# One decode step of cached attention and a gated MLP on one core: loops that stay rolled, an output projection in four column groups, and a first pass that does nothing

## The chip, the cores and the metric

The kernel runs on one core of a Trainium2 chip. The metric is device microseconds of one execution. The kernel before took 1302.17 us (median of three runs, 1301.73 to 1303.38). The profiled execution is a further one, and its own time stands beside its span below.

## The reference

Two sequences (B = 2) decode one token each. All numbers are float32.

```
h  = x + attention(layernorm(x)) @ wo        x: 2 x 448, 16 heads of 256
     q = layernorm(x) @ wq                   wq: 448 x 4096
     p = softmax(q . k_cache / 16)           k_cache, v_cache: 2 x 16 x 8192 x 256
     o = p @ v_cache                         wo: 4096 x 448
h2 = h + ((n @ w_gate) * (n @ w_up)) @ w_down    n = layernorm(h), F = 1792
```

The two caches are 537 MB of the 561 MB that have to be read, each byte once.

## The kernel before, in words

There are 32 turns, one for each pair of head and sequence. A turn's keys (8 MB) and values (8 MB) come by two DMAs that SyncE (SP) issues on one queue; 128 partitions hold 64 positions each. VectorE (DVE) multiplies keys by the query, which TensorE and ScalarE (ACT) have spread over the partitions, and sums each position (L334, L337), first 16 positions and then 48. TensorE (PE) transposes the maxima (L422), spreads the top (L426), adds up the exponentials (L431), spreads the query of a later turn (L270) and multiplies values by weights: 32 matmuls of 512 columns (`mix`, L413) whose outputs stand at partitions 0, 32, 64 and 96 in turn, which here are called four column groups. L438 turns the result into columns, and ACT writes it, scaled, into `oT`.

K is double buffered and V single. SP's order is fixed: the keys of turn i+1 go out when the maxima of turn i-1 are done (`m_in`), the values of turn i when the matmuls of turn i-1 are done (event "M"). On PE turns 0 to 30 are a hardware loop (`T.loop`); DVE, ACT and SP are written out turn by turn, and PE's 32nd turn and all that comes behind it are written out too.

The end is a chain. `project_out` multiplies `oT` of heads 0 to 14 by `wo` in two column halves (L493), part of it before and part behind the last turn's softmax. When the last values are in, head 15 follows: `o_sb` (L560), L438, `oT` (L563), eight matmuls into `h_ps` (L589), the mean, the centred residual `xr` (L630), the gate projection (L668, needs `wg`), the up projection in two halves (L668, `wu_a` and `wu_b`), their product (L717), transposes (L720, L727) and the down projection into `y_ps`, 14 chunks of four matmuls of 112 columns (L738), behind the four pieces of `wd`. Then a copy (L747) and the output DMA. The residual reaches `y_ps` by L523 and, for head 15, by L697.

Of the kernel before, what the change touches and what calls it, by code (L numbers as in the profile page):

```python
# [3 lines left out]
F32 = mybir.dt.float32  # L4
# [6 lines left out]
P = 128  # L11
HALF = 64
DC = 4
YN, YW = 4, D // 4
HW = D // 2
# [6 lines left out]
LASTV = 48  # L22
# [5 lines left out]
WIDE = [[min(n, (k + 1) * FH) - k * FH for n in FG] for k in range(2)]  # L28
PACKED = [3 * sum(n) + n[0] + n[2] for n in WIDE]
FF = [(n, g) for n in range(4) for g in range(4) if n < FG[g] // P]  # L30
DOWN = (5, 5, 3, 1)
# [8 lines left out]
class Line:  # L40


    def __init__(self, nc, engine, name):
        self.e = engine
        self.sem = nc.alloc_semaphore(name=name)
        self.n = 0
        self.seen = {}

    def wait(self, *tokens):
        for sem, n in tokens:  # L50
            if self.seen.get(sem.num, 0) < n:
                self.e.wait_ge(sem, n)
                self.seen[sem.num] = n

    def did(self, ins):
        ins.then_inc(self.sem, 1)
        self.n += 1
        return self.sem, self.n


class Tensor:


    def __init__(self, nc):
        self.e = nc.tensor
        self.sem = nc.alloc_semaphore(name="pe")
        self.n = 0
        self.parts = [(None, [])]

    def loop(self, *turns):  # L70

        self.parts.append((turns or None, []))

    def do(self, make, *waits, inc=False):
        self.parts[-1][1].append((make, waits, inc))
        if inc:
            self.n += 1
            return self.sem, self.n

    def emit(self):  # L80
        for turns, ops in self.parts:
            if turns:
                with self.e.Fori(*turns) as turn:
                    self.emit_part(ops, turn)
            else:
                self.emit_part(ops, None)

    def emit_part(self, ops, turn):
        seen = {}
        for make, waits, inc in ops:  # L90
            for w in waits:
                sem, n = w[:2]
                if len(w) == 3:
                    self.e.wait_ge(sem, turn * w[2] + n)
                elif seen.get(sem.num, 0) < n:
                    self.e.wait_ge(sem, n)
                    seen[sem.num] = n
            ins = make() if turn is None else make(turn)
            if inc:
                ins.then_inc(self.sem, 1)  # L100


def decode_block(nc, x, k_cache, v_cache, wq, wo, wg, wu, wd, out):
# [6 lines left out]
    bank = [nc.alloc_psum_tensor(f"bank{i}", [P, 512], F32)[:] for i in range(8)]  # L110
    first_sem = nc.alloc_semaphore(name="dve_first")
    V = Line(nc, nc.vector, "dve")
    A = Line(nc, nc.scalar, "act")
    A_q = Line(nc, nc.scalar, "act_q")
    G = Line(nc, nc.gpsimd, "pool")
    S = Line(nc, nc.sync, "sp")
    T = Tensor(nc)

# [11 lines left out]

    room = {"at": 2 * NF * D}

    def late(*shape):

        n = 1
        for k in shape[1:]:
            n *= k
        at = room["at"]
        room["at"] += -(-n // 8) * 8
        assert room["at"] <= NJ * DH  # L140
        got = k_flat[1][: shape[0], at : at + n]
# [15 lines left out]
    xr = sb("xr", P, DC + 1, B, 16)  # L157
    xz = sb("xz", P, DC + 1, B)
    sel = sb("sel", P, 2)
    rep = sb("rep", P, 2, B, REP)  # L160
    q_sb = sb("q_all", B, H * DH)

    s_x, s_wq, s_k0 = landing("x"), landing("wq"), landing("k0")
    s_k = [landing("k_even"), landing("k_odd")]
    s_v, s_v2 = landing("v"), landing("v_last")
    s_wo = [landing("wo_a"), landing("wo_b")]
    s_wg, s_wu = landing("wg"), [landing("wu_a"), landing("wu_b")]
    s_wd = [landing(f"wd{i}") for i in range(len(DOWN))]
    s_out = landing("out")

    def keys_of(cache, i, lo, hi):
        h, b = divmod(i, B)
        return cache[b, h].rearrange("(p j) d -> p j d", p=P)[:, lo:hi, :]

    x_in = load(A, x_sb, x.rearrange("b s d -> (b s) d"), s_x)
    wq_t = v_flat[:, : 3 * H * DH + H * DH // 2]
    wq_in = load(S, wq_t, wq, s_wq)
    k0_in = load(S, k_sb[0][:, :HC], keys_of(k_cache, 0, 0, HC), s_k0)  # L180
    k_in = {0: load(S, k_sb[0][:, HC:], keys_of(k_cache, 0, HC, NJ), s_k[0])}
    k_in[1] = load(S, k_sb[1], keys_of(k_cache, 1, 0, NJ), s_k[1])

    zero = G.did(nc.gpsimd.memset(ident, 0.0))
    G.wait(zero)
    ident_in = G.did(
        nc.gpsimd.affine_select(
            out=ident, in_=ident, compare_op=ALU.not_equal, fill=1.0, base=0,
            pattern=[[-1, P]], channel_multiplier=1,
        )  # L190
    )
    G.did(nc.gpsimd.memset(xz, 0.0))
    zeros_in = G.did(nc.gpsimd.memset(xr[:, DC - 1 :], 0.0))
# [12 lines left out]
    V.wait(t)
    xc_sb = sb("xc", B, DC * P)
    t = V.did(nc.vector.tensor_scalar(xc_sb[:, :D], x_sb, xmean, None, op0=ALU.add))
    V.wait(t)
    xc_in = V.did(nc.vector.tensor_copy(xc_sb[:, D:], xc_sb[:, D - HALF : D]))  # L210
    xq = o_sb[:B, :D]
    t = V.did(nc.vector.tensor_mul(xq, xc_sb[:, :D], xc_sb[:, :D]))
    V.wait(t)
    xvar = sb("xvar", B, 1)
    var_in = V.did(nc.vector.tensor_reduce(xvar, xq, axis=AX.X, op=ALU.add))

    std = sb("std", B, 1)
    A.wait(var_in)
    std_in = A.did(nc.scalar.activation(std, xvar, AF.Sqrt, bias=eps_t, scale=1.0 / D))
    rstd = sb("rstd", B, 1)  # L220
    V.wait(std_in)
    rstd_in = V.did(nc.vector.reciprocal(rstd, std))
    A.wait(rstd_in)
    A.did(nc.scalar.activation(std, std, AF.Exp, scale=0.0))

    xT_ps = bank[3][:, : DC * B].rearrange("p (c b) -> p c b", b=B)
    for c in range(DC):
        xT_in = T.do(
            lambda c=c: nc.tensor.transpose(
                xT_ps[:, c, :], xc_sb[:, c * P : (c + 1) * P], ident[:B, :B]  # L230
            ),
            ident_in, xc_in, inc=c == DC - 1,
        )
    V.wait(xT_in, zeros_in)
    for rows, c, to in LAYOUT:
        xz_in = V.did(nc.vector.tensor_copy(xz[rows, to], xT_ps[rows, c]))

    V.wait(ident_in)
    V.did(
        nc.vector.tensor_reduce(  # L240
            sel, ident.rearrange("p (g r) -> p r g", r=32)[:, :2, :], axis=AX.X, op=ALU.add
        )
    )
    V.did(
        nc.vector.tensor_copy(
            rep,
            ident.rearrange("p (k b) -> p k b", k=2)[:, :, :B, None].to_broadcast([P, 2, B, REP]),
        )
    )
    for ps in (o_ps, h_ps, bank[4][:, :HW]):  # L250
        set_in = V.did(nc.vector.memset(ps, 0.0))

    q_sel = sb("q_sel", B, DH)
    qb = [sb(f"qb{i}", P, DH) for i in range(2)]
    qb_ps = bank[1][:, :DH]
    q_ps = [bank[7][:B, :], bank[4][:B, :]]
    qsel_in, qb_in, Q_in = {}, {}, {}

    def select(i):
        h, b = divmod(i % NQ, B)  # L260
        if i > 0:
            A.wait(Q_in[i - 1])
        qsel_in[i] = A_q.did(
            nc.scalar.activation(  # L264
                q_sel, q_sb[:, h * DH : (h + 1) * DH], AF.Copy, scale=ident[:B, b : b + 1]
            )
        )

    def spread_query(*_):
        return nc.tensor.matmul(qb_ps, ones[:B, :], q_sel, start=True, stop=True)  # L270

    def take_query(i):
        A.wait(Q_in[i])
        qb_in[i] = A_q.did(nc.scalar.activation(qb[i % 2], qb_ps, AF.Copy))  # L274

    q_in = {}
    for g in range(NG):
        for c in range(DC):
            xs = c if c < DC - 1 else c + g // (NG // 2)
            at = c * H * DH + (g * QG if c < DC - 1 else g % (NG // 2) * QG)  # L280
            done = T.do(
                lambda g=g, c=c, xs=xs, at=at: nc.tensor.matmul(  # L282
# [11 lines left out]
        if g == 0:  # L294
            A.wait(q_in[0])
            select(0)
        if g == 1:
            Q_in[0] = T.do(spread_query, qsel_in[0], set_in, inc=True)
# [519 lines left out]
```

## Time and profile before

| | |
|---|---|
| median of three runs | 1302.17 us |
| profiled execution | 1301.42 us, span 1300.1 us |
| busy: DVE, PE, ACT | 1131.2, 470.6, 81.5 us |
| 16 DMA engines, mean busy share | 99.7% on the data queue |
| PE's granted clock, mean | 0.64 |

The profile's chain of waits gives 74% of the span to DMA and 25% to PE, nearly all of the latter `mix`. A timeline row has start and length in us, engine, line, operation, tiles, shapes and count; a float32 matmul is two records. In brackets stands how long the engine had been idle, and what ended that.

### The profile page before, as it was taken

The page shows a single profiled execution, that of the slowest core. Times are in us where ns is not written, and L with a number is a line of the kernel's source. Part 1 is how long each engine was busy: PE and PEld are TensorE (multiplying, and loading weights), DVE is VectorE, ACT ScalarE, POOL GpSimd, SP SyncE. Part 2 cuts the span into 40 slices and gives each one's busy share as a digit, 9 for nine tenths or more (in the row PEclk, how much of TensorE's full clock was granted, in tenths as well). Part 3 has the DMA queues.
Part 4 walks back from the last instruction along what each step waited for, and adds up shares of the span by engine and source line. Part 5 has one row for each costly group of instructions (what it writes and reads, how often), then busy time and mean ns, then how long its engine had stood idle before and what let it go on. Part 6 is the DMA issues. An engine that isn't in the chain of part 4 may idle for free.

```text
span 1300.1 us, 6914 instructions
## 1 busy us (share of the span) xinstructions
PE 470.6 (36%) x2992; PEld 155.1 (12%) x2992; DVE 1131.2 (87%) x266; ACT 81.5 (6%) x239; POOL 0.8 (0%) x8
## 2 busy tenths in 40 slices
PE   3643224333323433322333322333321333432387
PEld 0111011101001101101101101101100110110123
DVE  1999998889888889888889988888988888988861
ACT  1100000000000000000000000000000000000000
POOL 0000000000000000000000000000000000000000
PEclk9866566666556666556666656666656666655689
DMA  9999999999999999999999999999999999999998
GB/s 411 427 450 421 450 421 444 426 436 436 421 450 421 448 423 448 423 446 425 442 427 427 444 421 450 422 446 425 446 423 446 425 440 429 427 444 423 446 421 367
DMA packets 10973, 561.31 MB, mean 432 GB/s; under 512 B 1234, under 2 KB 1364, under 8 KB 1492
## 3 DMA queue, kind: packets, MB, share of 16 engines
q1 hardware_dynamic: 10960, 561.19, 99.7%
q8 instruction: 5, 0.08, 0.0%
q14 instruction: 4, 0.03, 0.0%
q10 hardware_dynamic: 4, 0.00, 0.0%
HBM read 561.19 MB, written 0.00 MB: 432 GB/s over the span
## 4 chain that ended last, share of the span: by engine, by line
DMA 74%; PE 25%; issue 0%; ACT 0%; SPq 0%; DVE 0%
DMA v<-in_A_v_cache_dram 71%; PE bank L413 22%; PE bank L282 2%; DMA v<-in_wd_dram 2%; DMA v<-in_wq_dram 1%; PE bank L270 0%; SPq L123 0%; PE bank L738 0%; ACT q_all L290 0%; ACT q_sel L264 0%; DVE k L747 0%; ACT qb L274 0%
## 5 line engine op out<-in xcount | busy, mean ns | idle before, releaser
L334 DVE TENSOR_TENSOR k<-k,qb 128x4096 f32<-128x4096 f32 x64 | 555.3, 8676 | 124.2 <-DMA k<-in_A_k_cache_dram 95.9
L337 DVE TENSOR_REDUCE s<-k 128x16 f32<-128x4096 f32 x64 | 555.2, 8675 | 1.1
L413 PE MATMUL bank<-v,p 128*2 128x512 f32 x2048 | 291.4, 733 | 342.9 <-DMA v<-in_A_v_cache_dram 342.9
L413 PEld LDWEIGHTS bank<-v,p 128*2 128x2 f32 x2048 | 53.6, 96 | 573.4 <-DMA v<-in_A_v_cache_dram 365.9
L426 PE MATMUL bank<-nm,row 1*128 1x1 f32 x64 | 18.4, 354 | 227.6 <-DVE nm L343 227.6
L422 PE MATMUL bank<-ident,m 128*1 128x128 f32 x32 | 11.8, 368 | 184.4 <-DVE m L381 184.4
L363 ACT ACTIVATE o_sb<-bank 128x512 f32<-128x512 f32 x31 | 18.5, 597 | 604.0 <-PE bank L413 604.0
L426 PEld LDWEIGHTS bank<-nm,row 1*128 1x128 f32 x64 | 15.6, 302 | 236.9 <-DVE nm L343 236.9
L438 PE MATMUL bank<-sel,o_sb 128*128 128x1 f32 x256 | 33.7, 253 | 23.3 <-ACT o_sb L363 22.5
L270 PE MATMUL bank<-q_sel,ones 2*128 2x256 f32 x66 | 39.0, 691 | 1.4 <-ACT q_sel L264 1.4
L438 PEld LDWEIGHTS bank<-sel,o_sb 128*128 128x128 f32 x256 | 31.0, 191 | 53.1 <-ACT o_sb L363 51.5
L282 PE MATMUL bank<-v,xz 128*2 128x512 f32 x64 | 30.7, 639 | 16.0 <-DMA v<-in_wq_dram 16.0
L352 ACT ACTIVATE nb<-bank 128x1 f32<-128x1 f32 x32 | 5.5, 171 | 441.5 <-PE bank L426 441.5
L431 PE MATMUL bank<-lsum,ones 128*128 128x1 f32 x64 | 18.5, 359 | 23.5 <-ACT p L355 23.5
L422 PEld LDWEIGHTS bank<-ident,m 128*1 128x1 f32 x32 | 2.5, 79 | 188.2 <-DVE m L381 187.8
L431 PEld LDWEIGHTS bank<-lsum,ones 128*128 128x128 f32 x64 | 15.8, 306 | 26.2 <-ACT p L355 26.2
L270 PEld LDWEIGHTS bank<-q_sel,ones 2*128 2x128 f32 x66 | 15.9, 297 | 3.7 <-ACT q_sel L264 2.4
L264 ACT ACTIVATE q_sel<-q_all,ident 2x256 f32<-2x256 f32 x33 | 16.2, 492 | 0.0
L274 ACT ACTIVATE qb<-bank 128x256 f32<-128x256 f32 x32 | 12.2, 382 | 54.5 <-PE bank L270 54.5
L493 PE MATMUL bank<-k,oT 128*2 128x224 f32 x120 | 13.4, 387 | 0.0
L343 DVE TENSOR_REDUCE nm<-bank 1x1 f32<-1x128 f32 x32 | 8.7, 272 | 4.4 <-PE bank L422 4.4
L597 DVE TENSOR_REDUCE k<-bank 128x1 f32<-128x128 f32 x1 | 0.3, 292 | 13.1 <-PE bank L589 13.1
(81 smaller groups left out, 97.3 us busy)
## 6 DMA issues: line engine op xcount, KB each, us to landing
v<-in_wq_dram SPq DMA_DIRECT2D x1, 7168.0 KB, 19.5
k<-in_wo_dram SPq DMA_DIRECT2D x2, 3584.0 KB, 35.3
k<-in_A_k_cache_dram SPq DMA_DIRECT2D x1, 6144.0 KB, 38.0
v<-in_A_v_cache_dram SPq DMA_DIRECT2D x1, 6144.0 KB, 21.6
k<-in_wg_dram SPq DMA_DIRECT2D x1, 3136.0 KB, 28.0
v<-in_wd_dram SPq DMA_DIRECT2D x2, 1120.0 KB, 18.0
k<-in_A_k_cache_dram SPq DMA_DIRECT2D x1, 2048.0 KB, 23.9
v<-in_A_v_cache_dram SPq DMA_DIRECT2D x1, 2048.0 KB, 26.1
```

The source lines that it names most:

```text
L264: nc.scalar.activation(q_sel, q_sb[:, h * DH : (h + 1) * DH], AF.Copy, scale=ident[:B, b : b + 1])
L270: return nc.tensor.matmul(qb_ps, ones[:B, :], q_sel, start=True, stop=True)
L282: lambda g=g, c=c, xs=xs, at=at: nc.tensor.matmul(q_ps[g % 2], xz[:, xs, :], wq_t[:, at : at + QG], start=(c == 0), stop=(c == DC - 1),),
L334: t = V.did(nc.vector.tensor_mul(kt, kt, q[:, None, :].to_broadcast([P, hi - lo, DH])))
L337: V.did(nc.vector.tensor_reduce(s_t[i % 2][:, lo:hi], kt, axis=AX.X, op=ALU.add)),
L363: osb_in[i] = A.did(nc.scalar.activation(o_sb, o_ps, AF.Copy))
L413: lambda *_, t=t, g=g: nc.tensor.matmul(o_ps[g : g + 2, :], p_t[:, 2 * t : 2 * t + 2], v_sb[:, 2 * t : 2 * t + 2, :], start=(t < 4), stop= ...
L422: return T.do(lambda *_: nc.tensor.transpose(mT_ps, m_t, ident), m, inc=True)
L426: lambda *_: nc.tensor.matmul(nb_ps, row, nm, start=True, stop=True), nm_done, inc=True
L431: lambda *_: nc.tensor.matmul(l_ps, ones, lsum, start=True, stop=True), p_done, inc=True
L438: lambda *_, c=c, k=k: nc.tensor.matmul(oT_ps[:, c : c + 1], o_sb[:, (2 * k + c) * P : (2 * k + c + 1) * P], sel[:, k : k + 1], start=(k = ...
L493: lambda h=h, c=c, k=k: nc.tensor.matmul(acc_ps[HALF * k : HALF * k + B, :], oT[:, h, c, :], wo_c[:, h, c, k * HW : (k + 1) * HW], start=F ...
```

## The change

1. An `Engine` class replaces `Line` and `Tensor`: work is listed with the names it waits for, and loops are emitted rolled. DVE: 15 passes of two turns; ACT: 16 passes of two; PE: 32 turns, with the work of the last turn behind branches inside the loop (`only`); the query projection: 4 passes of two groups.
2. PE, DVE and ACT each put their program into a loop of two passes, of which the first branches over everything (`early`, with a branch hint at the back edge). On PE that loop ends behind the gate projection, on the other two at the program's end.
3. Output projection: `acc_ps` is 448 wide, head h goes to column group h % 4. `wo` is one DMA, not two. Head 15 goes into the same bank; ACT copies the sum out with a running total, and four matmuls with `sel` add the groups while they transpose. The separate `h_ps` path, L523 and L697 are gone.
4. The up projection is whole, its two halves of product, transpose and copy follow it. `wu` is cut by rows and not by columns.
5. Down projection: the first ten chunks are 448 wide in column groups (`part_ps`); DVE adds them to the residual (`both`), and four matmuls with `rep` bring that into `y_ps` between chunk 11 and chunk 12. `wd` comes in five pieces and not four, and waits for the whole of the last `mix` and not for its first three quarters.

```diff
+    def emit(self, known):
+        seen = {}
+        if self.split:
+            with self.nc.Fori(0, 2, 1, engines=[self.e.engine], hint_back_edge=True) as go:
+                with self.e.If(go > 0):
+                    self.emit_ops(self.items[: self.split], known, seen)
+        self.emit_ops(self.items[self.split :], known, seen)
...
-DOWN = (5, 5, 3, 1)
+DOWN = (5, 5, 2, 1, 1)
+NPART, OPEN_AFTER = 10, 11
...
+    scores(0)
+    V.roll(1, NQ - 1, 2, lambda i: (scores(i), scores(i + 1)))
+    scores(NQ - 1)
...
+    A.roll(0, H, 1, act_turn)
...
+    def project_out(heads, *waits, done=None):
+        for c in range(2):
+            for h in heads:
+                g = 32 * (h % 4)
+                T.do(
+                    lambda h=h, c=c, g=g: nc.tensor.matmul(
+                        acc_ps[g : g + B, :], oT[:, h, c, :], wo_c[:, h, c, :],
+                        start=(h < 3 and c == 0), stop=(h >= H - 4 and c == 1),
...
+            project_out(range(0, 4), "wo", ("oT", H - 1))
...
+    project_out([H - 1], ("oT", NQ - 1), done="acc")
+    A.do(
+        lambda: nc.scalar.activation(sums[:, :D], acc_ps, AF.Copy, accum_out=total),
...
+                xc_ps[:, c, :], sums[:, c * P : (c + 1) * P], sel, start=(c == 0), stop=False
...
+    project(g_ps, wg_t, lambda c: "wg", "g", "g_blank", variance)
+    T.early()
...
+    project(u_ps, wu_t, lambda c: ("wu", c // 2), "u", "u_blank")
...
+                part_ps[32 * (k % 4) : 32 * (k % 4) + B, :],
+                hmT[:, j, 32 * g : 32 * (g + 1) : REP], wd_t[:, k, :],
...
+        lambda: nc.vector.tensor_tensor(both, part_ps, sums[:, :D], op=ALU.add),
```

PE between the 31st turn's end and the last `mix`, before: the projection of heads 0 to 7 (L493) waits for the first half of `wo`.

```order
L438 MATMUL bank<-sel,o_sb 128x1 [waits act] x4
L83 REGISTER_ALU
L83 COMPARE_AND_BRANCH
L482 MATMUL bank<-x,ident 2x224 x2
L493 MATMUL bank<-k,oT 2x224 [waits act,wo_a]
```

The same place now, inside the loop (L121 is the branch, L528 the projection, L557 the transposed maxima).

```order
L121 COMPARE_AND_BRANCH
L540 MATMUL bank<-x,ident 2x448
L528 MATMUL bank<-k,oT 2x448 [waits act0,wo]
L528 MATMUL bank<-k,oT 2x448 x15
L121 UNCONDITIONAL_BRANCH
L140 ISA
L557 MATMUL bank<-ident,m 1x128 [waits dve0]
```

The projection has half as many matmuls, twice as wide, and waits for all of `wo`; the last turn's softmax (from L557) still stands behind it.

PE behind the last `mix`, before: L438 to the first matmul of the gate projection.

```order
L438 MATMUL bank<-sel,o_sb 128x1 [waits act]
L438 MATMUL bank<-sel,o_sb 128x1 x3
L589 MATMUL bank<-k,oT 2x128 [waits act]
L589 MATMUL bank<-k,oT 2x128 x7
L613 MATMUL bank<-k,ones 128x8 [waits dve]
L620 MATMUL bank<-ident,k 128x8 [waits act]
L668 MATMUL bank<-k,xr 32x512 [waits dve,wg]
```

The same place now: L581 is the old L438, L528 head 15, L605 the sum over column groups, L615 the mean, L662 the gate projection.

```order
L581 MATMUL bank<-sel,o_sb 128x1 [waits act0]
L581 MATMUL bank<-sel,o_sb 128x1 x3
L106 REGISTER_ALU
L106 COMPARE_AND_BRANCH
L528 MATMUL bank<-k,oT 2x448 [waits act0]
L528 MATMUL bank<-k,oT 2x448
L605 MATMUL bank<-sel,k 128x2 [waits act0]
L605 MATMUL bank<-sel,k 128x2 x2
L605 MATMUL bank<-sel,k 128x2 [waits dve0]
L615 MATMUL bank<-k,ones 128x8 [waits dve0]
L662 MATMUL bank<-k,xr 32x512 [waits dve0,wg]
```

Eight narrow matmuls in four column groups became two wide ones in one group, and the two small ones behind them became five.

## Rows read from the trace of the kernel before

**Rows 1.** The page: data queue, packets, MB, share of 16 engines.
```profile
q1 hardware_dynamic: 10960, 561.19, 99.7%
```
**Rows 2.** Waits, 100 to 1200 us: total us, times, longest us.
```profile
PE bank L413 <- DMA v<-in_A_v_cache_dram: 316.3, 28, 12.0
DVE k L334 <- DMA k<-in_A_k_cache_dram: 92.3, 27, 3.9
```
**Rows 3.** DMA issues, whole span: count, median us from issue to landing.
```profile
k<-in_A_k_cache_dram SPq DMA_DIRECT2D x31, 42.1
v<-in_A_v_cache_dram SPq DMA_DIRECT2D x31, 29.5
```
**Rows 4.** Timeline of the head: `wq` is in, and the first values go out.
```profile
20.32 9.78 PE L282 MATMUL bank<-v,xz 128*2 128x512 f32 x16 [16.02 <-DMA v<-in_wq_dram]
53.66 0.33 SPq L123 DMA_DIRECT2D v<-in_A_v_cache_dram  x1
```
**Rows 5.** DMA queues, 100 to 1200 us: the only packets of code.
```profile
q14 instruction: 4, 0.03, 0.0%
```
**Rows 6.** DMA queues, 1240 to 1301 us: packets of code on PE's queue.
```profile
q8 instruction: 4, 0.07, 0.4%
```
**Rows 7.** Timeline of the end, from the last but one `mix`.
```profile
1238.73 9.86 PE L413 MATMUL bank<-v,p 128*2 128x512 f32 x64 [11.63 <-DMA v<-in_A_v_cache_dram]
...
1250.78 7.91 PE L493 MATMUL bank<-k,oT 128*2 128x224 f32 x64
...
1260.67 5.46 PE L493 MATMUL bank<-k,oT 128*2 128x224 f32 x56
...
1270.35 7.05 PE L413 MATMUL bank<-v,p 128*2 128x512 f32 x64 [3.11 <-DMA v<-in_A_v_cache_dram]
...
1277.46 0.60 ACT L560 ACTIVATE o_sb<-bank 128x512 f32<-128x512 f32 x1 [17.15 <-PE bank L413]
...
1279.20 0.26 ACT L563 ACTIVATE oT<-bank,rl 128x2 f32<-128x2 f32 x1 [1.14 <-PE bank L438]
...
1279.52 0.62 PE L589 MATMUL bank<-k,oT 128*2 128x128 f32 x16 [0.35 <-ACT oT L563]
...
1280.75 0.39 PE L613 MATMUL bank<-k,ones 128*128 128x8 f32 x2 [0.61 <-DVE k L604]
...
1281.40 0.57 DVE L630 COPY xr<-bank 128x96 f32<-128x96 f32 x3 [0.60 <-PE bank L620]
...
1282.58 0.20 PEld L668 LDWEIGHTS bank<-k,xr 128*32 128x32 f32 x8 [1.31 <-DMA k<-in_wg_dram]
1282.59 3.29 PE L668 MATMUL bank<-k,xr 128*32 128x512 f32 x16 [1.22 <-DVE k L643]
...
1286.12 1.91 PE L668 MATMUL bank<-k,xr 128*32 128x512 f32 x16
...
1291.37 1.06 PE L668 MATMUL bank<-k,xr 128*32 128x256 f32 x16
...
1292.51 0.42 DVE L717 TENSOR_TENSOR k<-bank,k 128x256 f32<-128x256 f32 x1 [0.61 <-PE bank L668]
1292.99 0.44 PE L720 MATMUL bank<-ident,k 128*128 128x128 f32 x2 [0.56 <-DVE k L717]
...
1296.95 0.97 PE L738 MATMUL bank<-v,k 128*32 128x112 f32 x32 [0.46 <-DMA v<-in_wd_dram]
1298.00 0.28 DVE L747 COPY k<-bank 128x112 f32<-128x112 f32 x1 [4.11 <-PE bank L738]
```
**Rows 8.** Windows of the end: busy us of each engine, PE's granted clock, DMA share, GB/s.
```profile
1270.00:1272.00 2.00, 1.65 (x16) 0.42 (x20) 0.00 (x0) 0.00 (x0) 0.00 (x0) 1.00 1.01 434
1282.00:1284.00 2.00, 1.41 (x10) 0.69 (x14) 0.88 (x5) 0.00 (x0) 0.00 (x0) 0.50 1.04 444
...
1295.00:1296.00 1.00, 0.67 (x28) 0.68 (x32) 0.00 (x0) 0.00 (x0) 0.00 (x0) 1.00 0.69 274
1296.00:1297.00 1.00, 0.54 (x26) 0.30 (x19) 0.00 (x0) 0.00 (x0) 0.00 (x0) 1.00 0.29 113
```

More of the change, by code (lines that the diff above doesn't have):

```diff
@@ L37 @@
 )
[L40 to L84, printed above, removed]
-            else:
[L86 to L100, printed above, removed]
@@ L168, in decode_block @@
[L168 to L181, printed above, removed]
@@ L223, in decode_block @@
[L223 to L236, printed above, removed]
@@ new lines, in decode_block @@
+    G.do(lambda: nc.gpsimd.memset(xz, 0.0))
+    G.do(lambda: nc.gpsimd.memset(xr[:, DC - 1 :], 0.0), done="blanks")
+    for t, value in ((eps_t, EPS), (ones, 1.0), (avg, 1.0 / D), (row, DH**-0.5)):
+        V.do(lambda t=t, value=value: nc.vector.memset(t, value))
+    V.do(
+        lambda: nc.vector.tensor_reduce(xsum, x_sb, axis=AX.X, op=ALU.add), "x", done="xsum"
+    )
+    V.do(
+        lambda: nc.vector.tensor_scalar(xmean, xsum, -1.0 / D, None, op0=ALU.mult),
+        "xsum", done="xmean",
+    )
@@ new lines, in decode_block, with spread_query @@
+    V.do(
+        lambda: nc.vector.tensor_reduce(
+            sel, ident.rearrange("p (g r) -> p r g", r=32)[:, :2, :], axis=AX.X, op=ALU.add
+        ),
+        "ident", done="sel",
+    )
+    V.do(
+        lambda: nc.vector.tensor_copy(rep, sel[:, :, None].to_broadcast([P, B, REP])), "sel"
+    )
+    zeroed = (o_ps, part_ps, acc_ps)
+    for ps in zeroed:
+        V.do(lambda ps=ps: nc.vector.memset(ps, 0.0), done="set" if ps is acc_ps else None)
+    GH = NG // 2
+    def spread_query(i, name="Q"):
+        T.do(
+            lambda *_: nc.tensor.matmul(qb_ps, ones[:B, :], q_sel, start=True, stop=True),
+            ("qsel", i), done=(name, i),
+        )
@@ new lines, in project_groups @@
+    def project_groups(t):
+        for k in range(2):
+            for c in range(DC):
+                xs, base = (c, c * H * DH + k * GH * QG) if c < DC - 1 else (c + k, c * H * DH)
+                T.do(
+                    lambda turn, k=k, c=c, xs=xs, base=base: nc.tensor.matmul(
+                        q_ps[k], xz[:, xs, :], wq_t[:, bass.ds(turn * QG + base, QG)],
+                        start=(c == 0), stop=(c == DC - 1),
+                    ),
+                    *([("q", 2 * (t - 1) + k)] if c == 0 else []),
+                    done=("qp", 2 * t + k) if c == DC - 1 else None,
+                )
+        T.only(t == 0, spread_query, 0, "Q0")
@@ L402, in every, with collect @@
-    def every(tokens):
-        sem, n = tokens[0]
-        by = tokens[1][1] - n
-        assert all(tokens[i] == (sem, n + by * i) for i in range(TURNS)), tokens
-        return sem, n, by
-    def mix(lo, hi, landed):
+            ),
+            ("nb", i), done=("p", i),
+        )
+    def collect(i, turn_of):
+        b = i % B
+        A.do(lambda *_: nc.scalar.activation(o_sb, o_ps, AF.Copy), ("M", i), done=("osb", i))
+        A.do(
+            lambda turn: nc.scalar.activation(
+                oT[:, bass.ds(turn_of(turn), 1), :, b], oT_ps[:, None, :], AF.Copy, scale=rl
+            ),
+            ("O", i), ("rl", i), done=("oT", i),
+        )
@@ L410, in mix, with act_turn @@
+    def act_turn(h):
+        for b in range(B):
+            i = h * B + b
+            exponentials(i)
+            take_query(i + 2)
+            select(i + 3, lambda turn, b=b: (turn + (b + 3) // B) & (H - 1))
+            collect(i, lambda turn: turn)
+    A.roll(0, H, 1, act_turn)
+    def mix(i, lo, hi, *waits, done=None):
         for t in range(lo // 2, hi // 2):
             g = 32 * (t % 4)
-            done = T.do(
+            T.do(
                 lambda *_, t=t, g=g: nc.tensor.matmul(
@@ new lines, in heads_out, with hold, tensor_turn @@
+    def heads_out(k):
+        if k == 0:
+            T.do(
+                lambda: nc.tensor.matmul(
+                    acc_ps[3 * 32 : 3 * 32 + B, :], ident[:B, :B], x_sb, start=True, stop=False
+                )
+            )
+            project_out(range(0, 4), "wo", ("oT", H - 1))
+            project_out(range(4, 8))
+        else:
+            project_out(range(8, 12), ("oT", NQ - 3))
+            project_out(range(12, H - 1))
+    def hold(*waits):
+        T.do(None, *waits)
+    def tensor_turn(i):
+        last = i == NQ - 1
+        T.only(last, heads_out, 0)
+        T.do(
+            lambda *_: nc.tensor.transpose(mT_ps, m_t, ident), ("m", i), done=("T", i)
+        )
+        T.do(
+            lambda *_: nc.tensor.matmul(nb_ps, row, nm, start=True, stop=True),
+            ("nm", i), done=("N", i),
+        )
+        T.do(
+            lambda *_: nc.tensor.matmul(l_ps, ones, lsum, start=True, stop=True),
+            ("p", i), done=("L", i),
+        )
+        spread_query(i + 2)
+        T.only(last, heads_out, 1)
+        at = 0
+        for k, n in enumerate(LAST):
+            if k > 0:
+                T.only(last, hold, ("v_last", k))
+            mix(
+                i, at, at + n, *([("v", i)] if k == 0 else []),
+                done=("M", i) if k == len(LAST) - 1 else None,
+            )
+            at += n
@@ L545, in decode_block @@
-    last["M"] = mix(LASTV, NJ, v2_in)
-    S.wait(mixed_a)
-    wd_t = v_flat[:, : NF * D].rearrange("p (n d) -> p n d", d=D)
-    wd_in, at = {}, 0
-    for k, cnt in enumerate(DOWN):
-        got = load(
-            S, wd_t[:, at : at + cnt, :].rearrange("p n d -> p (n d)"),
-            wd[:, at * D : (at + cnt) * D], s_wd[k],
-        )
-        for j in range(at, at + cnt):
-            wd_in[j] = got
-        at += cnt
-    A.wait(last["M"])
-    osb_in[n] = A.did(nc.scalar.activation(o_sb, o_ps, AF.Copy))
@@ L627, in decode_block @@
+            "sums", *(["sums_d"] if c == DC - 1 else []),
+        )
+    V.do(
+        lambda: nc.vector.tensor_mul(mean, share, total[:, None, :].to_broadcast([P, DC, B])),
+        "sums", "share", done="mean",
+    )
+    T.do(
+        lambda: nc.tensor.matmul(xc_ps, ones, mean, start=False, stop=True), "mean", done="xc_h"
+    )
     for rows, c, to in LAYOUT:
         k = rows.stop - rows.start
-        xr_in = V.did(
-            nc.vector.tensor_copy(
+        V.do(
+            lambda rows=rows, c=c, to=to, k=k: nc.vector.tensor_copy(
@@ new lines, in decode_block @@
+    down_of = [k for k, n in enumerate(DOWN) for _ in range(n)]
+    for k, (j, g) in enumerate(FF[:NPART]):
+        T.do(
+            lambda k=k, j=j, g=g: nc.tensor.matmul(
+                part_ps[32 * (k % 4) : 32 * (k % 4) + B, :],
+                hmT[:, j, 32 * g : 32 * (g + 1) : REP], wd_t[:, k, :],
+                start=(k < 4), stop=(k >= NPART - 4),
+            ),
+            ("hmT_in", j // 2), ("wd", down_of[k]), done="part" if k == NPART - 1 else None,
+        )
+    both = late(P, D)
@@ L722, in product, with open_sum @@
+    V.do(
+        lambda: nc.vector.tensor_tensor(both, part_ps, sums[:, :D], op=ALU.add),
+        "part", "sums", done="both",
+    )
+    def open_sum():
+        for q in range(DC):
+            T.do(
+                lambda q=q: nc.tensor.matmul(
+                    y_ps[32 * q : 32 * q + 32, :], rep.rearrange("p b r -> p (b r)"),
+                    both[:, q * W : (q + 1) * W], start=False, stop=False,
                 ),
-                t, inc=j == 1,
+                "both",
             )
-        V.wait(flipped)
@@ new lines, in decode_block @@
+        if k == OPEN_AFTER:
+            open_sum()
+    y = late(P, W)
+    V.do(lambda: nc.vector.tensor_copy(y, y_ps), "y", done="y_in")
+    s_out = landing("out")
+    load(S, out, y[::REP, :], s_out, "out", "y_in")
+    S.do(lambda: nc.sync.sem_clear(range(first_sem.num, s_out.num)))
+    S.do(lambda: nc.sync.sem_clear(s_out), "out")
+    engines = (S, A, G, V, T)
+    for e in engines:
+        e.count(known)
+    known["all_q"] = known["qp", NG - 1]
+    A.early()
+    V.early()
+    for e in (S, G, T, A, V):
+        e.emit(known)
```

828 lines of the change are left out of this document (371 added, 457 removed).

## The prediction

> **What bounds the kernel now.** I read the DMA part of the page first, because the chain of waits is three quarters DMA. The data queue kept the 16 engines busy for 99.7% of the span [rows 1], and 561.19 MB in 1300.1 us are 0.432 MB a us. Next come the waits of the steady part: per turn PE waits 11.3 us for values (316.3 / 28) and DVE 3.4 us for keys (92.3 / 27) [rows 2]. Then the issues, which say whether the queue ever runs dry: 8.39 MB need 19.4 us, yet values land 29.5 us after their issue and keys 42.1 us after theirs [rows 3]. So a value DMA stands 10 us, a key DMA 23 us behind other data, and the stream doesn't notice an engine that is later by less. In such a kernel a change can act in three places only: before the stream starts, on the stream's own length, and behind its last byte. The end is read from the timeline [rows 7] and from the windows [rows 8].
>
> **Steady turns.** Rolled loops add register instructions for waits and a branch per pass. No row prices them. Their cover is DVE's 3.4 us a turn, 6.8 us a pass of two turns, and PE's 11.3 us; ACT is busy 81.5 us in all. A row bounds them from above in kind: PE ran 31 passes of such a loop, and its only long waits in it are for data [rows 2]. Lower end 0, upper end (refetched code) is a rival below; I take 0, nearest to PE's loop. Writing out fewer turns removes nothing that anyone waited for either.
>
> **Head.** The empty passes, the new order on DVE and the register addresses of the query projection all lie before or in a stretch with cover: PE stands idle 16.0 us until `wq` lands at 20.32 [rows 4]. Behind it the price of lateness is the first values' issue at 53.66: 7.34 + 16.78 MB are ahead of it, which at 0.432 MB a us plus about 2 us of start end near 58, so some 4 us are free, less the lead that a transfer needs. The 32 matmuls stay the same; one of the two query spreads goes behind them. I take 0; an empty pass would have to cost over 16 us, or the loop over 3 us, to show.
>
> **Stream.** Bytes are the same. `wo` in one piece saves one DMA, the fifth piece of `wd` adds one: nothing. `wd` now waits for all of the last `mix`, some 2 us later; 6.4 MB of `wg` and `wu` are ahead of it, 14.8 us, so its place in the queue is free. One thing can change. In the last 61 us PE's queue brought four packets of code that took 0.4% of 16 engines, so 3.9 us or 1.0 us of one engine each [rows 6]; an engine that carries one is late with its own data for good. And the engines do end raggedly: shares of 0.69 and 0.29 in the last two us [rows 8]. If the empty pass loads the tail's code early, up to (1 - 0.69) + (1 - 0.29) = 1.0 us can come back. If early packets only move the lateness, 0. I take 0 and keep -1.0 as a bound, because the early packets fall on the same engines' first data.
>
> **Behind the last turn's keys.** The projection of heads 0 to 7 started at 1250.78, on the first half of `wo` [rows 7]. It now waits for the whole. `wo` is complete when the last values' first part starts: 6.29 MB take 14.6 us and were used at 1270.35, so 1255.7. Its 16 matmuls of 448 columns run in four column groups, as `mix` does: 7.05 us for 32 of 512 is 0.22 each, 0.19 for 448 columns, 3.1 us; at the low clock at most double, 6.2. The softmax behind it keeps the 2.0 us between the two L493 rows, the extra query spread costs up to 1.2, and 14 more matmuls 2.7 to 5.3. PE is ready between 1264.2 and 1270.4; the values were used at 1270.35. Hidden, though its upper end just touches.
>
> **From the last values to the gate projection.** This is the path. `o_sb` to `oT` keeps its instructions (+0.1 for a register address). Head 15: eight matmuls in four groups took 0.62; now two of 448 columns stand in one group, one behind the other, so 4 x 0.19 = 0.75 each, 1.5 us at the full clock and 3.0 at the low one: +0.9 to +2.4. The copy of the sum is 448 columns and a running total where before a total and a 128-column copy ran in a row: `o_sb`, 512 columns, takes 0.60, so 0.6 to 0.8 against 0.6: 0 to +0.2. Four matmuls with `sel` are what L438 is (1.14 us that `oT` waited), then one of 0.39, against the old stretch from 1280.75 to 1281.40: +0.6 to +0.9. The three copies to `xr` stay. Sum: +1.6 to +3.6, likeliest +1.9, so `xr` is ready at 1281.97 + 1.9 = 1283.9. Before, the gate projection started at 1282.59, held by `wg`. It is late by 1.3 us, bounds 1.0 and 3.0.
>
> **From there to the end.** The gate projection took 5.4 us, from 1282.59 to 1288.03, at 0.50 in its first half [rows 7, 8]. Now to 1289.3. L697's eight matmuls on PE are gone, and the up projection is 16 matmuls at about 0.22, 3.5 us: 1292.8, against 1292.43 before (1291.37 + 1.06). `wu`'s second half was needed near 1290 before and is no later. Then both products (0.42 each), transposes (0.44) and copies (0.42): the first copy is done 1.5 us after the up projection, the second 2.0. Ten chunks at 0.19 take 1.9 us from 1294.3 to 1296.3; DVE adds 448 columns, 0.42 x 448 / 256 = 0.7, to 1297.0; the four `rep` matmuls and the last eight cost 0.5 to 0.7: 1297.7. Before, PE ended at 1297.92, after a wait of 0.46 for `wd` [rows 7]. So compute arrives when the data does: the last chunk can't start before its piece lands near 1297.3, and the end stays at 1297.9, -0.5 to +2.0. The final copy (0.28) and the output DMA stay.
>
> The sum is 0: the profiled execution would again take 1301.4, of which 1300.1 are span. It lay 0.75 below the median of the runs, and that spread (1301.73 to 1303.38) is as large as my terms; I put the forecast on the median, 1302.2.
>
> **Rivals.** *The clock falls before the last `mix` (slower).* PE had paused 3.1 us and still had 1.00 when the values came [rows 7, 8]. In the new order PE's work behind the softmax may end near 1267 or earlier, with no L523 work behind it, so the pause may be longer. A steady `mix`, which begins at the low clock after 11.6 us of pause, took 9.86 against 7.05 [rows 7]: +2.8. No wait is left in the chain to absorb it, except the 0.2 us above, and head 15 at the low clock adds up to 1.5. Price +1.8 to +4, centre +2.4: 1304.6. It decides from a pause at which the granted clock has gone to 0.50. For it: after the quiet stretch ahead of 1282 the clock did fall. Against it: the pause may be no longer, and a slower last `mix` is possible before as well, so part of it is in the old median. Chance 0.22.
>
> *The engines' ragged end is evened out.* -1.0 at the last landing, if compute is also early enough (full clock in the gate projection saves 3.29 - 1.91 = 1.4). 1301.2. Chance 0.17.
>
> *Loops fetch their code again.* If every back edge did, 16 on ACT, 15 on DVE and 31 on PE bring 62 packets of 1.0 us on 16 engines: 3.9 us on the stream, 1306.1, and more where a stall exceeds 6.8 us a pass on DVE. Against it: while PE's loop turned 28 times, between 100 and 1200 us, its queue brought no packet at all [rows 5]. [...] This trace doesn't show it for PE, and none shows a loop on ACT or DVE. It decides if a loop doesn't stay loaded. Chance 0.04.
>
> *Faster by more than the ragged end holds.* I see no mechanism; 0.02 for one that I have missed.
>
> **How the numbers follow.** The forecast, no change within a microsecond, has 0.55. Taking 0.2% (2.6 us) as what a measurement of this kernel can tell from none: the slow clock passes it in about a third of its cases, 0.08; with refetching 0.04 slower has 0.12. Faster has 0.03, same 0.85. The range, from 1300.8 (ragged end) to 1304.9 (slow clock, most of it), leaves out about 0.15. The likeliest case's own range is 1301.2 to 1303.2.
>
> **What would show it.** Right: the data queue near 99.7%, `mix` still waiting about 11 us for values, no code packets in the steady part; `xr` near 1284, so that `wg` no longer ends PE's wait there; the last down matmuls on `wd` or within a microsecond of it. Wrong: a DVE wait for something other than keys, a share of the data queue under 99%, a last PE matmul that ends behind 1299 with its clock at 0.50 in the last `mix`, or an end before 1296.5.

## The result

The changed kernel took 1303.59 us (median of 22 runs, 1301.72 to 1307.58), the kernel before beside it 1301.76 (22 runs, 1301.35 to 1303.38). The ratio is 1.0015, 95% interval 1.0008 to 1.0021: slower by 0.15%, inside the 0.2% that the prediction took as no change, but clear of noise. The spread tells more than the median. Nine of the 22 executions lie between 1301.7 and 1302.3, where most of the kernel before lie (18 of 22 are under 1302.4); six between 1303.0 and 1304.6; seven between 1306.1 and 1307.6. The profiled execution is one of the last: 1306.09 us, span 1304.8.

First the rows that answer to [rows 1, 2] and the wait that [rows 4] showed: data queue and q8 (page; read as PE's code queue, as four of its five packets in the kernel before came behind 1240 [rows 6], where PE leaves its loop near 1250), the only row of the DMA queues from 100 to 1200 us, waits from 100 to 1200 us, and the start.

```profile
q1 hardware_dynamic: 10960, 561.19, 99.4%
q8 instruction: 2, 0.03, 0.0%
```
```profile
q1 hardware_dynamic: 8193, 477.17, 100.1%
```
```profile
PE bank L515 <- DMA v<-in_A_v_cache_dram: 318.8, 28, 11.6
...
DVE k L426 <- DMA k<-in_A_k_cache_dram: 95.1, 27, 3.8
```
```profile
2.22 0.06 DVE L297 MEMSET eps<- 2x1 f32 x1 [2.22 <-issue]
...
7.86 0.55 PE L328 MATMUL bank<-ident,xc 2*128 2x2 f32 x4 [7.86 <-issue]
...
21.68 9.24 PE L366 MATMUL bank<-v,xz 128*2 x16 [13.27 <-DMA v<-in_wq_dram]
...
52.28 0.33 SPq L167 DMA_DIRECT2D v<-in_A_v_cache_dram  x1
```

The same in the kernel before: PE's code queue (page), and the first work of DVE and PE.

```profile
q8 instruction: 5, 0.08, 0.0%
```
```profile
0.79 0.06 DVE L195 MEMSET eps<- 2x1 f32 x1 [0.79 <-PEq L800]
...
3.74 0.56 PE L229 MATMUL bank<-ident,xc 2*128 2x2 f32 x4 [3.74 <-DVE xc L210]
```

The steady part is what it was: PE waits 11.4 us a turn for values, DVE 3.5 us for keys, and no queue but the data queue moved anything. The empty passes are to be seen at the start. PE's first matmul comes at 7.86 and not at 3.74, and `wq` is used 1.4 us later, but the first values go out 1.4 us earlier than before, at 52.28. None of this reaches the end: the last values are used at 1270.33 (1270.35 before). The whole 4.7 us of this execution lie behind that. Its end, against [rows 7]:

```profile
1255.80 4.45 PE L528 MATMUL bank<-k,oT 128*2 128x448 f32 x32 [4.35 <-DMA k<-in_wo_dram]
...
1262.87 3.18 PE L528 MATMUL bank<-k,oT 128*2 128x448 f32 x28
...
1270.33 9.57 PE L515 MATMUL bank<-v,p 128*2 128x512 f32 x64 [4.29 <-DMA v<-in_A_v_cache_dram]
...
1279.98 0.60 ACT L490 ACTIVATE o_sb<-bank 128x512 f32<-128x512 f32 x1 [16.24 <-PE bank L515]
...
1282.20 3.10 PE L528 MATMUL bank<-k,oT 128*2 128x448 f32 x4 [0.52 <-ACT oT L492]
...
1287.34 0.56 DVE L620 COPY xr<-bank 128x96 f32<-128x96 f32 x3 [1.07 <-PE bank L615]
...
1288.04 2.62 PE L662 MATMUL bank<-k,xr 128*32 128x512 f32 x16 [0.74 <-DVE xr L620]
...
1291.11 6.03 PE L662 MATMUL bank<-k,xr 128*32 128x512 f32 x48
...
1302.02 0.57 PE L739 MATMUL bank<-v,k 128*32 128x112 f32 x16
1302.65 0.27 DVE L749 COPY k<-bank 128x112 f32<-128x112 f32 x1 [0.91 <-PE bank L739]
```

And windows of it (engines' busy us, PE's granted clock, DMA share, GB/s), against [rows 8]:

```profile
1270.00:1272.00 2.00, 1.67 (x9) 0.26 (x13) 0.00 (x0) 0.00 (x0) 0.00 (x0) 0.50 0.99 426
...
1282.00:1284.00 2.00, 1.80 (x3) 0.34 (x4) 0.00 (x0) 0.15 (x1) 0.00 (x0) 0.57 0.94 401
...
1290.00:1292.00 2.00, 2.00 (x12) 0.93 (x14) 0.32 (x2) 0.00 (x0) 0.00 (x0) 0.50 1.02 430
...
1296.00:1297.00 1.00, 1.00 (x8) 0.11 (x2) 0.00 (x0) 0.00 (x0) 0.00 (x0) 1.00 0.17 54
```

Read along the path. The last `mix` took 9.57 us and not 7.05, at 0.50 up to 1275 where it had been at 1.00: 2.5 us. Head 15 took 3.10 and not 0.62, again near the low clock (0.57 from 1282 to 1284): `xr` was done at 1287.90, 5.9 us later than before. The gate projection waits for `xr` now (0.74) and not for `wg`, and it runs at 0.50 in its middle (1290 to 1292). `wd` went out 4.2 us later than before, behind the slow `mix` (1279.97 against 1275.74), but hardly any data is left to come at 1297, as before (18 GB/s from 1297 to 1298, 4 before), while PE works on to 1302.59. The low clock costs because in this execution nothing behind the last values waits for data any more: from 1280 on no wait of PE, DVE or ACT ends on a DMA.

### The profile page after: what moved, and what is told of

It is laid out like the page before. It is cut to its first block, busy times and chain, and to the rows that moved or that the text cites. A ratio compares the mean times of both kernels' runs of the same rounds, so it can differ in the third digit from the quotient of the medians.

```text
span 1304.8 us, 7298 instructions
## 1 busy us (share of the span) xinstructions
PE 470.4 (36%) x2806; PEld 149.1 (11%) x2806; DVE 1131.7 (87%) x264; ACT 83.6 (6%) x245; POOL 0.8 (0%) x8
## 4 chain that ended last, share of the span: by engine, by line
DMA 73%; PE 26%; issue 0%; DVE 0%; ACT 0%; ACTq 0%
DMA v<-in_A_v_cache_dram 71%; PE bank L515 23%; PE bank L366 2%; DMA v<-in_wq_dram 2%; PE bank L662 1%; PE bank L528 0%; PE bank L712 0%; PE bank L581 0%; PE bank L605 0%; ACT k L596 0%; DVE k L721 0%; PE bank L357 0%; ACT o_sb L490 0%; DVE xr L620 0%; PE bank L739 0%
## 5 line engine op out<-in xcount | busy, mean ns | idle before, releaser
L557 PE MATMUL bank<-ident,m 128*1 128x128 f32 x32 | 11.8, 369 | 175.3 <-DVE m L448 175.3
L581 PE MATMUL bank<-sel,o_sb 128*128 128x1 f32 x256 | 33.7, 253 | 23.3 <-ACT o_sb L490 23.3
L581 PEld LDWEIGHTS bank<-sel,o_sb 128*128 128x128 f32 x256 | 31.0, 191 | 53.1 <-ACT o_sb L490 53.1
L366 PE MATMUL bank<-v,xz 128*2 x64 | 30.0, 630 | 13.3 <-DMA v<-in_wq_dram 13.3
L557 PEld LDWEIGHTS bank<-ident,m 128*1 128x1 f32 x32 | 2.5, 79 | 179.0 <-DVE m L448 178.2
L394 ACT ACTIVATE q_sel<-q_all,ident 2x256 f32 (+1 forms) x35 | 17.2, 492 | 0.0
L528 PE MATMUL bank<-k,oT 128*2 128x448 f32 x64 | 10.7, 651 | 4.9 <-DMA k<-in_wo_dram 4.4
```

What stands on the lines that cost most here:

```text
L366: lambda turn, k=k, c=c, xs=xs, base=base: nc.tensor.matmul(q_ps[k], xz[:, xs, :], wq_t[:, bass.ds(turn * QG + base, QG)], start=(c == 0), ...
L394: return nc.scalar.activation(q_sel, q_sb[:, bass.ds(at, DH)], AF.Copy, scale=ident[:B, b : b + 1])
L557: lambda *_: nc.tensor.transpose(mT_ps, m_t, ident), ("m", i), done=("T", i)
L581: lambda *_, c=c, k=k: nc.tensor.matmul(oT_ps[:, c : c + 1], o_sb[:, (2 * k + c) * P : (2 * k + c + 1) * P], sel[:, k : k + 1], start=(k = ...
```

## The experiments

Theory A: the loss is PE's clock. Theory B: the chain behind the last values is too long at any clock. Theory C: loops or empty passes cost. The kernels of one round ran on one chip with the kernel before (median 1301.9 to 1302.1).

**Idle matmuls ahead of the last mix.** Nothing reads what they write.

```diff
             project_out(range(12, H - 1))
+            fill(6)     # matmul(bank[6][:, 256:512], ident, wo_c[:, 0, 0, :256])
```

> The changed kernel with six matmuls of 256 columns into an unused part of a PSUM bank, behind the last turn's projection and ahead of the last mix; nothing waits for them. Theory A (the loss is PE's clock: in part of the executions it has fallen to 0.50 when the last values land): the slow executions (1306 to 1307.6) vanish, every one is near 1301.7 to 1303, median about 1302.0; last mix about 7 us. Theory B (the longer chain behind the last values costs by itself): median stays near 1303.6. Theory C (loops or the empty passes cost): stays near 1303.6.

Measured: 1303.85 (1301.94 to 1305.93). The timeline of its profiled execution (1303.83):

```profile
1270.56 7.05 PE L515 MATMUL bank<-v,p 128*2 128x512 f32 x64
...
1279.89 3.15 PE L528 MATMUL bank<-k,oT 128*2 128x448 f32 x4 [0.52 <-ACT oT L492]
...
1285.79 2.98 PE L672 MATMUL bank<-k,xr 128*32 128x512 f32 x16 [0.74 <-DVE xr L630]
```

The mix ran at the full clock (7.05 us) and the executions above 1306 are gone, but head 15 took 3.15 us, the first half of the gate projection 2.98, and the median stayed. Theory A in its first form, with the pause ahead of the mix as the cause, fell: here the clock was at 0.50 behind a full mix (1280 to 1282).

**Head 15 in four column groups.**

```diff
-    project_out([H - 1], ("oT", NQ - 1), done="acc")
+    for c in range(2):
+        for k in range(2):      # group 2c+k takes half k of the columns
+            matmul(acc_ps[32*(2*c+k):..., k*224:(k+1)*224], oT[:, 15, c, :], wo_c[:, 15, c, k*224:...])
```

> The changed kernel with head 15 as four matmuls of 224 columns in four column groups at once, in place of two of 448 in one group: 1.1 us less on PE at the full clock, 2.3 us less at the low one. Theory A: executions with a fast last mix don't move (1301.7: they end on the last wd piece), those with a slow one gain 1 to 2.3 us (from 1307 to about 1305), median about 1302.5. Theory B: every execution gains about 1.1 us, median about 1302.4, lowest under 1301. Theory C: the median gains 1 us or nothing, and the spread of the executions stays.

Measured: 1302.61 (1301.69 to 1305.78). The lowest executions didn't move, the highest lost 1.8 us. That is theory A's row; B wanted every execution lower. With 11 runs of such a spread the median's fall of 1 us is weak evidence by itself. In the profiled execution (1304.44) the mix took 10.01 us and head 15 only 0.56.

**A longer quiet stretch.** Heads 8 to 14 ahead of the softmax.

```diff
             project_out(range(4, 8))
-        else:
             project_out(range(8, 12), ("oT", NQ - 3))
             project_out(range(12, H - 1))
```

> The changed kernel with the projection of heads 8 to 14 moved ahead of the last turn's softmax, so that PE has only a few short matmuls between about 1263 and the last values at 1270.3. Theory A: the clock falls in nearly every execution, last mix 9.5 us or more, all near 1306 to 1307.5. Theory B and C: no change, median 1303.6 with the same spread, as no wait on the path is longer.

Measured: 1305.55 (1301.86 to 1307.42): five of twelve near 1302, seven above 1305.4. The median rose by 2 us with no longer wait on the path, as A wanted and B and C did not; but "nearly every execution" was wrong: the share near 1302 is that of the unedited kernel (9 of 22), only the executions in between are gone. At so few runs this decides little. Its profiled execution, at 1302.12, shows more:

```profile
1270.00 8.95 PE L515 MATMUL bank<-v,p 128*2 128x512 f32 x64 [3.32 <-DMA v<-in_A_v_cache_dram]
...
1281.25 1.67 PE L528 MATMUL bank<-k,oT 128*2 128x448 f32 x4 [0.52 <-ACT oT L492]
...
1285.66 1.91 PE L660 MATMUL bank<-k,xr 128*32 128x512 f32 x16 [0.74 <-DVE xr L618]
```

The mix was slow there, but head 15 (1.67) and the gate projection (1.91) took no longer than with the clock held (the fifth experiment), and most of the 2 us was won back: the down projection's wide chunks, the last of which start there at 1295.03 after a wait of 0.39 for `wd`, ran through here from 1294.67 to 1296.72. A mix at the low clock alone is nearly covered in this kernel (PE ended at 1298.61, against 1298.20).

**Without the empty passes.**

```diff
-    T.early()
-    A.early()
-    V.early()
```

> The changed kernel without the empty first passes on PE, DVE and ACT. Theory A: median within 0.5 us of 1303.6 and the same two kinds of executions; code packets come at the loop's end instead of at the start, PE's first matmul back near 3.7 us. Theory C: 1 us or more less if the passes cost, or more if code now arrives late behind the loops (an idle time put down to issue at the tail).

Measured: 1304.25 (1301.76 to 1307.83), inconclusive at this spread; it is settled below. PE's first matmul is back at 3.74. In the profiled execution (1304.50) the mix ran at the full clock (7.05), but head 15 took 2.69 us and the first half of the gate projection 3.63, so the low clock comes without empty passes too.

**The clock held.** Six idle matmuls as above, and five more in PE's short waits behind the mix (one ahead of L581, one ahead of head 15, one behind it, two ahead of the gate projection).

> The changed kernel with the six idle matmuls ahead of the last mix and five more (256 columns, about 0.43 us each at the full clock) in PE's short waits behind it: ahead of L581, ahead of head 15, behind it, and two ahead of the gate projection. The first round showed that six ahead of the mix alone only move the low clock to head 15 and the gate projection. Theory A2 (the changed chain from the last values to the output has no slack left, so each stretch at 0.50 in it is paid): with the clock kept at 1.00 all executions lie within 0.8 us of 1301.9. Theory B (the chain is too long even at the full clock): median 1303 or more, all executions late alike.

Measured: 1302.23 (1301.70 to 1303.22), ratio 1.0002 (0.9993 to 1.0011). The profiled execution, 1301.70:

```profile
1269.80 7.05 PE L515 MATMUL bank<-v,p 128*2 128x512 f32 x64 [1.36 <-DMA v<-in_A_v_cache_dram]
...
1279.13 1.67 PE L528 MATMUL bank<-k,oT 128*2 128x448 f32 x4
...
1282.84 0.56 DVE L634 COPY xr<-bank 128x96 f32<-128x96 f32 x3 [1.07 <-PE bank L628]
...
1283.70 1.91 PE L676 MATMUL bank<-k,xr 128*32 128x512 f32 x16
...
1295.03 1.29 PE L726 MATMUL bank<-v,k 128*2 128x448 f32 x9 [0.39 <-DMA v<-in_wd_dram]
...
1297.42 0.40 PE L743 MATMUL bank<-k,rep 128*32 128x112 f32 x8 [0.33 <-DVE k L735]
...
1297.63 0.57 PE L753 MATMUL bank<-v,k 128*32 128x112 f32 x16
```

Eleven matmuls that compute nothing take away the executions above 1303.3; ten of the eleven lie under 1302.5, as A2 wanted, one at 1303.22. PE waits for `wd` again. The longer chain is still there, and it isn't wholly covered: the last matmuls wait for DVE's sum (0.33) and not for `wd`, and PE ends at 1298.20, 0.3 us behind the kernel before (1297.92). So the clock is the cause of most of the loss; what the length costs by itself is some tenths of a us, not clear of noise.

The profiled executions side by side, in us:

| execution | last mix | head 15 | gate projection, first half | PE's last matmul ends |
|---|---|---|---|---|
| before, 1301.42 | 7.05 | 0.62 | 3.29 | 1297.92 |
| clock held, 1301.70 | 7.05 | 1.67 | 1.91 | 1298.20 |
| longer quiet stretch, 1302.12 | 8.95 | 1.67 | 1.91 | 1298.61 |
| idle matmuls ahead of the mix, 1303.83 | 7.05 | 3.15 | 2.98 | 1300.33 |
| head 15 in four groups, 1304.44 | 10.01 | 0.56 | 3.38 | 1300.91 |
| without empty passes, 1304.50 | 7.05 | 2.69 | 3.63 | 1301.01 |
| changed kernel, 1306.09 | 9.57 | 3.10 | 2.62 | 1302.59 |

With the longer chain, the late ones of these executions are those in which the work behind the mix, too, meets the low clock.

**The same with the narrow head 15.**

> The same with head 15 as four matmuls of 224 columns in four column groups. Theory A2: 1301.5 to 1301.9, at or just below the kernel before, since the last wd piece then sets the end. Theory B: 1.1 us under the run without it, about 1302 or more.

Measured: 1302.14 (1301.70 to 1303.70). No gain from 1.1 us less on PE, and above the row of A2 (1301.5 to 1301.9). The profiled execution, 1302.35:

```profile
1289.65 1.91 PE L685 MATMUL bank<-k,xr 128*32 128x512 f32 x16 [1.16 <-DMA k<-in_wu_dram]
...
1295.53 1.29 PE L735 MATMUL bank<-v,k 128*2 128x448 f32 x9 [0.79 <-DMA v<-in_wd_dram]
...
1297.23 0.62 DVE L744 TENSOR_TENSOR k<-bank,k 128x448 f32<-128x448 f32 x1 [3.88 <-PE bank L735]
1297.91 0.40 PE L752 MATMUL bank<-k,rep 128*32 128x112 f32 x8 [0.34 <-DVE k L744]
```

The time saved went into the waits for `wu` and `wd`; behind them stands DVE's sum.

**The kernel before, made late.** Five idle copies on ACT.

```diff
     hq = late(P, P)
+    for _ in range(5):
+        A.wait(A.did(nc.scalar.activation(o_sb, o_sb, AF.Copy)))
```

> The kernel before with five idle copies on ACT (128 x 512 in SBUF, about 0.55 us each) between oT and the copy of h_ps: the residual xr is ready about 1.8 us later, as in the changed kernel, and nothing else is different. Theory A2: the slack of the old chain covers a part; median 0.5 to 1.5 us above the kernel before, with executions spread up to 1305, because its gate projection, too, runs partly at 0.50. Theory B (length alone): every execution 1.8 us less the 0.6 us for which xr waited for wg, so all 1.2 us later. Theory C (loops or empty passes are the cause): no more than 0.6 us, spread unchanged.

Measured: 1304.57 (1302.50 to 1305.80). The five copies took 3.26 us, so the delay is about 2.2. The profiled execution, 1305.80:

```profile
1270.54 9.80 PE L413 MATMUL bank<-v,p 128*2 128x512 f32 x64 [6.14 <-DMA v<-in_A_v_cache_dram]
...
1282.32 3.26 ACT L600 ACTIVATE o_sb<-o_sb 128x512 f32<-128x512 f32 x5
...
1287.30 3.63 PE L670 MATMUL bank<-k,xr 128*32 128x512 f32 x16 [0.76 <-DVE xr L632]
...
1299.43 2.89 PE L740 MATMUL bank<-v,k 128*32 128x112 f32 x112
```

Without the new loops, empty passes or a new projection, lateness alone makes the old kernel behave much like the changed one: executions spread over 3 us, and an end that waits for no data. Its last mix, too, can begin at the low clock (9.80 us). So the low clock doesn't need the change, which used up the slack that had covered it; whether the change also makes it more frequent these runs don't show. The median rose by 2.6 us, more than any theory's number, and the lowest execution by 1.0.

**The residual earlier.** The held and narrow kernel with five chunks in column groups, not ten, and the residual behind chunk 9.

```diff
-NPART, OPEN_AFTER = 10, 11
+NPART, OPEN_AFTER = 5, 9
```

> The changed kernel with the idle matmuls, head 15 in four groups, and the first five chunks of the down projection (one piece of wd) in column groups in place of ten, the residual brought in behind chunk 9 in place of chunk 11; so the sum on DVE is done before the last two pieces of wd land, and PE ends on the last piece. Theory A2 with a data floor: 0.3 to 0.7 us below the same kernel with ten chunks, so 1301.4 to 1301.8, as the last output matmuls then wait for wd alone. If the floor is elsewhere: no change from 1302.1.

Measured: 1301.44 (1301.13 to 1301.62), and 1301.53 (1301.08 to 1302.09) when it ran again:

> The kernel with the idle matmuls, the narrow head 15 and the residual brought in early, once more, so that the two below are compared with it on one chip: 1301.1 to 1301.7 again.

Both times the ratio is 0.9993 (0.9984 to 1.0002), 0.6 and 0.5 us below the kernel before, not clear of noise. Against the kernel with ten chunks, which ran on another chip, it is 0.7 us. The end of its first profiled execution, 1301.38:

```profile
1295.34 1.17 PE L762 MATMUL bank<-v,k 128*32 128x112 f32 x40 [0.82 <-DMA v<-in_wd_dram]
1296.32 0.38 PE L752 MATMUL bank<-k,rep 128*32 128x112 f32 x8
1296.51 1.37 PE L762 MATMUL bank<-v,k 128*32 128x112 f32 x32
1297.94 0.27 DVE L772 COPY k<-bank 128x112 f32<-128x112 f32 x1 [2.77 <-PE bank L762]
```

With ten chunks DVE's sum ran from 1297.23 to 1297.85 (the profiled execution of 1302.35 above), and the `rep` matmuls waited for it; now PE goes through without waiting for it.

**The kernel before with idle matmuls.** Nine of them, at the like places.

> The kernel before with nine idle matmuls of 256 columns at the like places (four ahead of the last mix, five in the waits behind it), into an unused part of another PSUM bank. Theory A2: its executions above 1302.5 vanish too and the median falls by 0.1 to 0.4 us; the lowest stay at 1301.4, set by the last wd piece. Theory B or C: no change in median or spread.

Measured: 1301.65 (1301.35 to 1302.84), ratio 0.9996 (0.9987 to 1.0005). The median fell by 0.4 and all executions but one lie under 1302, as A2 said, though the interval alone would not show it. Its profiled execution, 1301.46, shows the cover of the old chain at work:

```profile
1270.38 8.62 PE L413 MATMUL bank<-v,p 128*2 128x512 f32 x64 [3.66 <-DMA v<-in_A_v_cache_dram]
...
1283.98 1.91 PE L682 MATMUL bank<-k,xr 128*32 128x512 f32 x16
...
1296.99 0.97 PE L752 MATMUL bank<-v,k 128*32 128x112 f32 x32 [0.46 <-DMA v<-in_wd_dram]
```

The mix began at the low clock here as well (8.62 us), and the gate projection started 1.4 us later than in [rows 7]. But it then ran at the full clock (1.91), and PE waited 0.46 us for the last piece of `wd`, as there.

**Empty passes and a loop, priced.** On the kernel with the residual earlier, which is called tight here because its executions lie within about 1 us, once without the empty passes and once with DVE's 30 turns written out.

> The same without the empty first passes on PE, DVE and ACT. Its tight executions allow this edit to be priced, which the first round could not. Theory A2: within 0.4 us of the run with them. Theory C: 0.5 us or more below it if the passes cost, 0.5 us or more above it if code now comes late at the tail.

> The same with DVE's 30 looped turns written out (its empty first pass stays). Theory A2: within 0.4 us, DVE's wait for keys again about 3.4 us a turn. Theory C: 0.5 us or more below, if the loop costs.

Measured: 1301.27 (1301.03 to 1301.92) and 1301.20 (1301.11 to 1301.93), against 1301.53. Neither the passes nor DVE's loop cost or give more than about 0.3 us, which is not clear of noise. Theory C is out for these two; ACT's loop was not written out, but the old kernel made late shows the loss without it.

## Why the prediction was right, and where it was not

- *Bound by data, steady part free*: right. The waits per turn are 11.4 and 3.5 us, and no packet of code fell into the steady part. (PE's loop, [rows 2], also waits long for DVE's maxima, 162.3 us for L381 and 215.2 for L343 from 100 to 1200 in the kernel before, which the prediction left out.)
- *Head*: right; the empty pass delayed PE's first matmul by 4.1 us of the 16 that were free.
- *Stream*: two packets on PE's queue in the whole execution and not five, and no earlier end. The bound of -1.0 never showed as a time; without the passes the tight kernel is lower, if anything (1301.27 against 1301.53). That an engine stays late by a packet of code that it carries, and that the early packets fall on the same engines, was my estimate: no row tells one engine from another.
- *Projection behind the keys*: 4.45 and 3.18 us, in the bounds of 3.1 to 6.2 and 2.7 to 5.3, ready at 1266.1, hidden.
- *From the last values to `xr`*: +1.9 us at the full clock was forecast. With the clock held (the fifth experiment) the stretch from the end of the mix to `xr` is 1276.85 to 1283.40, 6.55 us, with three idle matmuls in it; before 1277.40 to 1281.97, 4.57: +2.0. Right. In the profiled execution 8.0 us were measured, +3.4, within the +3.6 of the bounds.
- *"So compute arrives when the data does"*: this is the step that failed, as a statement on most executions. It took the clock of the old execution for the new one: 1.00 in the mix, 0.50 only in half of the gate projection. With the clock held the sum is off by little: 1297.7 was forecast for PE's end and 1298.20 measured, with DVE's sum and not `wd` as the last wait. So little is left that the clock decides: it is at 0.50 in different stretches from one execution to the next. The profiled execution shows what the prediction itself had named as a sign of being wrong: a last PE matmul that ends behind 1299 (1302.59) with the clock at 0.50 in the last `mix`; and `xr` was ready at 1287.90, not near 1284.
- *The slow clock as a rival*: mechanism right, chance, place and size wrong. It had 0.22; 13 of 22 executions are above 1303. I placed it ahead of the last mix, with up to 1.5 us for head 15 and nothing for the gate projection. A slow mix by itself cost 0.4 us at the end (1298.61 against 1298.20), as waits for data further on still covered the rest, not at least 1.8; the idle matmuls ahead of the mix showed that head 15 and the gate projection decide. The profiled execution, with low clock in all three, spans 4.7 us more.
- *The number*: the forecast 1302.2 is that of the nine executions near 1302, which are the minority. The median 1303.59 lies past that case's own range (1301.2 to 1303.2) and inside the whole one, and its rise of 1.8 us is under the 2.6 us taken as no change. That it stayed inside the range is partly luck, as the median of such a spread falls where the share of late executions puts it: two edited kernels above have medians of 1304.25 and 1305.55, close to the upper bound of 1304.9 and past it.
- *Refetched code*: not seen. From 100 to 1200 us no queue carried a packet of code, while PE, DVE and ACT all turned in loops, so none of them fetched its code again there, where the rival counted a packet for every back edge. In the kernel before, with DVE and ACT written out, four packets came in that stretch [rows 5].

What stays open: what decides in a single execution where the clock falls. The experiments change how often it does and what it costs, and don't show this.

## What to carry to other kernels

This kernel waits for data up to its end, and the chain behind the last byte was nearly free as long as some of its waits still ended on data: with the clock held, 2.0 us more up to `xr` moved PE's end by 0.3 us. The edit that lengthened it left the fastest executions nearly alone (1301.72 against 1301.35) and still cost 1.8 us in the median, because it took the cover from what varied here, PE's clock. In another kernel of this kind, count the slack for the low clock that its own traces show; look at the spread of the runs and not only at their median; and try a few idle matmuls in PE's short waits before shortening the chain: eleven of them brought the median here from 1303.59 to 1302.23.

## What the hardware showed that I had not expected

In one profiled execution the granted clock fell to 0.50 within 2.4 us of a full mix that had run at 1.00. Windows of the execution with idle matmuls ahead of the mix only, columns as above:

```profile
1274.00:1277.00 3.00, 3.00 (x33) 0.73 (x28) 0.00 (x0) 0.00 (x0) 0.00 (x0) 1.00 1.03 443
1280.00:1282.00 2.00, 2.00 (x3) 0.25 (x2) 0.00 (x0) 0.00 (x0) 0.00 (x0) 0.50 0.92 392
```

The mix ended at 1277.61, head 15 began at 1279.89 and ran at 0.50, with only the eight short records of L581 in between. With five more idle matmuls, it was at 1.00 there:

```profile
1280.00:1282.00 2.00, 1.91 (x10) 0.77 (x7) 0.27 (x2) 0.63 (x2) 0.00 (x0) 1.00 0.90 385
1282.00:1284.00 2.00, 2.00 (x16) 1.48 (x19) 1.03 (x6) 0.00 (x0) 0.00 (x0) 1.00 1.00 430
```

Two wide matmuls in one column group cost 1.67 us at the full clock and 2.69 to 3.15 in the three profiled executions with low clock there; the same work in four groups cost 0.56, at the full clock. And the empty pass at the start put PE's first matmul 4.1 us and DVE's first instruction 1.4 us later (7.86 against 3.74, 2.22 against 0.79); without it (the fourth experiment) they came at 3.74 and 0.80.
